# Streaming the weights of an output projection through quarters of the PE array, and loading four of their rows on five DMA engines

## The chip, the cores and the metric

The kernel runs on one core of a Trainium2 chip. The metric is the device time of one execution in microseconds. Times are medians of several runs on one chip. The profile is of one execution, and its times count from the start of the profiled span, which is 1.7 to 1.9 us shorter than the device time of the same execution.

## The reference

Two branches share one input row `x` of 1024 values and are mixed by a gate. Branch A is attention with one query over a cache of 65,536 keys and values for 4 groups of heads; branch B is a small gated MLP. Both end in an output projection.

```python
# cut to what matters
q = x @ wq                                    # 32 heads of 128
o = softmax(q k^T / sqrt(128)) v              # 4 groups, 65536 keys each: 128 MB of K and V
a = o.reshape(4096) @ wo                      # wo: 4096 x 1024, 8 MB
b = (z1 * spatially_gated(z2)) @ w_out        # w_out: 1792 x 1024, 3.5 MB
out = g * a + (1 - g) * b                     # 1024 values
```

All inputs and the output are bf16. The kernel folds the gates into the vectors (`oa` for branch A, `uT` for branch B), so both projections accumulate into one PSUM tile.

## The kernel before

Everything is loaded by one DMA queue in program order, into five buffers of 32 KB per partition. The projection is the end of the kernel:

```python
    def load(src, shape, name):
        t = kv.tile([P, CT * P], BF16, name=name, tag="kv")     # five buffers
        ...
        nc.sync.dma_start(out=v, in_=src)
        return v
    # ... attention; the last group's V tiles, then:
    out_ps = pss.tile([P, NJ, W], FP32, name="out_ps", tag="spt")

    def project(w, n, vec, c0, first=False, last=False):
        w = w.rearrange("p c (m j) -> p c j m", j=NJ)           # NJ = 8
        for c in range(n):
            for j in range(NJ):
                nc.tensor.matmul(
                    out_ps[:, j, :], lhsT=w[:, c, j, :],        # 128 columns, every 8th
                    rhs=vec[:, c0 + c:c0 + c + 1].to_broadcast([P, W]),   # W = 64
                    start=(first and c == 0 and j == 0), stop=(last and c == n - 1),
                    skip_group_check=True)

    project(load(B_w_out..., (FC, D), "wout_t"), FC, uT, 0, first=True)   # FC = 14
    wo_view = A_wo.rearrange("(p c) n -> p c n", c=OC)          # OC = 32 rows a partition
    c0 = 0
    for split in WO_SPLIT:                                      # ((8, 8), (6, 4, 3, 2, 1))
        t = kv.tile([P, CT * P], BF16, name="wo_t", tag="kv")
        ...
        for n in split:
            nc.sync.dma_start(out=t[:, c0 - b:c0 - b + n, :], in_=wo_view[:, c0:c0 + n, :])
            project(t[:, c0 - b:c0 - b + n, :], n, oa, c0, last=(c0 + n == OC))
            c0 += n
    out_sb = const.tile([P, NJ], BF16, name="out_sb")
    nc.vector.tensor_copy(out=out_sb[:], in_=out_ps[:, :, 0])
    nc.sync.dma_start(out=out..., in_=out_sb[:])
```

Each partition holds 32 rows of `wo`, of 2 KB each. One such row in all 128 partitions is 256 KB; I call it a chunk. In the text above, "four rows" are four chunks, 1 MB.

## Time and profile before

| | before |
|---|---|
| device time, median | 394.09 us |
| span of the profile | 392.5 us |
| last `wo` transfer landed | 388.06 us |
| the cast after the last matmul starts | 389.96 us |
| from there to the end of the span | 2.54 us |

The page of the kernel before, in part. The row DMA gives in 40 slices of the span the mean busy share of the 16 DMA engines in tenths, GB/s what they moved; q8 is the queue that fetches instructions. In the lines of groups stand: line, engine, operation, tiles, shapes, count, then busy time in us and the mean ns of one, then the idle time before them.

```profile
span 392.5 us, 11905 instructions
...
DMA  8999999999999999999999999999999999999971
GB/s 331 435 429 441 426 424 432 432 427 422 424 440 427 426 422 431 424 432 429 426 427 431 429 436 428 426 426 432 432 427 429 429 427 427 429 431 428 412 328 73
...
q8 instruction: 43, 0.70, 0.7%
...
HBM read 162.01 MB, written 0.00 MB: 413 GB/s over the span
...
L430 PE MATMUL out_ps<-oa,wo_t 128*128 128x64 bf16 x256 | 15.7, 229 | 0.6 <-DMA wo_t<-in_A_wo_dram 0.6
L430 PEld LDWEIGHTS <-wo_t 128*128 128x128 bf16 x256 | 15.6, 171 | 0.7 <-DMA wo_t<-in_A_wo_dram 0.7
...
L449 DVE CAST out_sb<-out_ps 128x8 bf16<-128x8 f32 x1 | 0.2, 167 | 25.1 <-PE out_ps L430 25.1
```

The DMA is busy in every slice but the last two, at about 430 GB/s in most of them. The weight loads of the projection, of 128 columns that lie 16 bytes apart, take 171 ns each; those of adjacent columns take 100 to 104 ns here (100 for the scores, 101 for `kn`, 104 for `q`).

The end of the chain of waits of the kernel before (start in us, duration in us, engine, what, count):

```profile
336.97 41.19 DMA wo_t<-in_A_wo_dram
378.20 11.74 PE out_ps L430 x192
```

After a `wo` transfer landed at 378.16, PE worked off 192 matmuls from 378.20 on without a gap, 61 ns each, and ended at 389.94. So the last stage looks bound by PE. The table of stretches says that this is half of the truth. Its columns are: stretch and length in us; busy us (and count) of PE, of PE's weight loads, of DVE, ACT and POOL; the granted clock; the DMA share; GB/s.

```profile
368.00:373.00 5.00, 5.00 (x87) 5.00 (x86) 0.00 (x0) 0.00 (x0) 0.00 (x0) 0.66 1.00 419
373.00:378.00 5.00, 4.65 (x78) 4.54 (x76) 0.00 (x0) 0.00 (x0) 0.00 (x0) 1.00 0.98 408
378.00:380.00 2.00, 1.80 (x30) 1.80 (x31) 0.00 (x0) 0.00 (x0) 0.00 (x0) 0.57 0.64 259
380.00:382.00 2.00, 2.00 (x37) 2.00 (x36) 0.00 (x0) 0.00 (x0) 0.00 (x0) 0.58 0.55 223
382.00:384.00 2.00, 2.00 (x37) 2.00 (x36) 0.00 (x0) 0.00 (x0) 0.00 (x0) 1.00 0.50 206
384.00:386.00 2.00, 2.00 (x37) 2.00 (x36) 0.00 (x0) 0.00 (x0) 0.00 (x0) 1.00 0.48 185
386.00:388.00 2.00, 2.00 (x37) 2.00 (x36) 0.00 (x0) 0.00 (x0) 0.00 (x0) 1.00 0.10 39
388.00:390.00 2.00, 1.93 (x33) 1.82 (x31) 0.04 (x1) 0.00 (x0) 0.00 (x0) 1.00 0.00 0
```

From 378 on, only half of the DMA engines still work: the share is 0.5, at half the GB/s. The completion increments that the trace records for each transfer show the same: an ordinary transfer has sixteen, as many as the core has DMA engines, and I read them as one per engine. For the last chunk they come at 378.3 to 379.7 (seven engines), 382.5 (one), 385.9 to 386.4 (six) and 387.9 and 388.1 (two). An engine moves its 16 KB share of a chunk in 0.61 to 0.65 us; eight engines are simply late, by a lag that grows through the run (the increments of one transfer are 2.2 us apart at 49 us, 5.2 at 195 and 9.8 at the end). DMA therefore ends only 1.9 us before PE. Neither can be shortened alone by much.

### The profile page before, as it was taken

Reading aid. Unit: us, or ns where it says so; the run is one execution under the profiler, and the core shown is the slowest. Engines: PE = TensorE matmul, PEld = TensorE weight load, DVE = VectorE, ACT = ScalarE, POOL = GpSimd, SP = SyncE. Lnnn points to the kernel's source line nnn. Section 1 sums busy time; section 2 is a strip of 40 time slices with the busy share of each in tenths; the row PEclk is TensorE's granted clock in tenths of the full one; section 3 lists DMA queues with packets and bytes.
Section 4 is the critical chain, followed back from the end, with each engine's and each line's share of the span. In section 5 each row is a group of like instructions: output and inputs, shape, how many; then the busy total and the mean of one; then the engine's idle time right before and its main releaser. Section 6 shows DMA issues by size and latency. Waiting matters only on the chain.

```text
span 392.5 us, 11905 instructions
## 1 busy us (share of the span) xinstructions
PE 299.9 (76%) x5539; PEld 255.0 (65%) x5539; DVE 160.0 (41%) x316; ACT 122.2 (31%) x139; POOL 1.0 (0%) x9
## 2 busy tenths in 40 slices
PE   0774379887889985979884969689949797544697
PEld 0764379887888865857774858468738683311697
DVE  3011047574685541538551526367514357201100
ACT  1000036543594431424631423237404243100000
POOL 1000000000000000000000000000000000000000
PEclk9999999999999996999996989989978898955889
DMA  8999999999999999999999999999999999999971
GB/s 331 435 429 441 426 424 432 432 427 422 424 440 427 426 422 431 424 432 429 426 427 431 429 436 428 426 426 432 432 427 429 429 427 427 429 431 428 412 328 73
DMA packets 6566, 162.78 MB, mean 415 GB/s; under 512 B 884, under 2 KB 884, under 8 KB 1268
## 3 DMA queue, kind: packets, MB, share of 16 engines
q1 hardware_dynamic: 6480, 162.01, 96.6%
q8 instruction: 43, 0.70, 0.7%
q14 instruction: 7, 0.06, 0.0%
q10 hardware_dynamic: 36, 0.00, 0.0%
HBM read 162.01 MB, written 0.00 MB: 413 GB/s over the span
## 4 chain that ended last, share of the span: by engine, by line
DMA 50%; PE 42%; DVE 3%; issue 2%; ACT 1%; SPq 1%; DVEq 0%; ACTq 0%
DMA kn<-in_A_k_cache_dram 39%; PE tps L329 22%; DMA wo_t<-in_A_wo_dram 10%; PE spt L308 10%; PE o_ps L354 5%; PE out_ps L430 3%; DVE ktt L334 1%; DVE scT L291 1%; PE om_ps L372 1%; PE s_ps L362 1%; ACT scT L314 1%; ACT ktt L332 1%; SPq L85 0%; DVE o_sb L369 0%; PE nb_ps L286 0%
## 5 line engine op out<-in xcount | busy, mean ns | idle before, releaser
L329 PE MATMUL tps<-ident_b,kn 128*128 128x128 bf16 x2048 | 164.7, 226 | 37.3 <-DMA kn<-in_A_k_cache_dram 35.7
L329 PEld LDWEIGHTS <-kn 128*128 128x128 bf16 x2048 | 124.5, 101 | 62.8 <-DMA kn<-in_A_k_cache_dram 39.3
L334 DVE COPY ktt<-tps 128x1024 bf16<-128x1024 bf16 x171 | 116.4, 689 | 113.4 <-PE tps L329 112.6
L332 ACT COPY ktt<-tps 128x1024 bf16<-128x1024 bf16 x85 | 86.0, 1012 | 163.8 <-PE tps L329 163.8
L308 PE MATMUL spt<-qT,ktt 128*128 128x64 bf16 (+7 forms) x2048 | 104.0, 194 | 6.8 <-issue 6.7
L308 PEld LDWEIGHTS <-ktt 128*128 128x128 bf16 x2048 | 87.0, 100 | 8.4 <-issue 8.1
L354 PE MATMUL o_ps<-vt,scT 128*32 128x512 bf16 x512 | 51.9, 432 | 14.9 <-DMA vt<-in_A_v_cache_dram 14.9
L354 PEld LDWEIGHTS <-scT 128*32 128x32 bf16 x512 | 15.3, 100 | 26.7 <-issue 21.0
L314 ACT CAST scT<-spt 128x512 bf16<-128x512 f32 x32 | 18.8, 588 | 16.1 <-PE spt L308 16.1
L316 DVE TENSOR_TENSOR mxr<-scT,mxr 128x512 bf16<-128x512 bf16 x24 | 10.2, 426 | 20.3 <-ACT scT L314 18.9
L295 ACT ACTIVATE scT<-scT 128x1024 bf16<-128x1024 bf16 x16 | 16.4, 1059 | 4.9 <-DVE scT L291 4.9
L430 PE MATMUL out_ps<-oa,wo_t 128*128 128x64 bf16 x256 | 15.7, 229 | 0.6 <-DMA wo_t<-in_A_wo_dram 0.6
L430 PEld LDWEIGHTS <-wo_t 128*128 128x128 bf16 x256 | 15.6, 171 | 0.7 <-DMA wo_t<-in_A_wo_dram 0.7
L193 PE MATMUL z_ps<-xT,win_t 128*128 128x18 bf16 x224 | 13.7, 211 | 1.8 <-DMA win_t<-in_B_w_in_dram 1.3
L193 PEld LDWEIGHTS <-win_t 128*128 128x128 bf16 x224 | 13.7, 158 | 1.8 <-DMA win_t<-in_B_w_in_dram 1.4
L362 PE MATMUL s_ps<-scT,ones_b 128*32 128x512 bf16 x32 | 13.4, 418 | 0.0
L369 DVE COPY o_sb<-o_ps 128x512 f32<-128x512 f32 x4 | 2.7, 684 | 26.0 <-PE o_ps L354 26.0
L245 PE MATMUL q_ps<-xT,wq_t 128*128 128x1 bf16 x256 | 7.1, 165 | 7.6 <-DMA wq_t<-in_A_wq_dram 7.6
L245 PEld LDWEIGHTS <-wq_t 128*128 128x128 bf16 x256 | 7.0, 104 | 7.8 <-DMA wq_t<-in_A_wq_dram 7.8
L291 DVE TENSOR_TENSOR scT<-scT,negm 128x1024 bf16<-128x1024 bf16 x16 | 10.7, 683 | 0.2
L449 DVE CAST out_sb<-out_ps 128x8 bf16<-128x8 f32 x1 | 0.2, 167 | 25.1 <-PE out_ps L430 25.1
L430 PE MATMUL out_ps<-uT,wout_t 128*128 128x64 bf16 x112 | 6.9, 235 | 3.2 <-DMA wout_t<-in_B_w_out_dram 3.2
(87 smaller groups left out, 57.0 us busy)
## 6 DMA issues: line engine op xcount, KB each, us to landing
kn<-in_A_k_cache_dram SPq DMA_DIRECT2D x16, 4096.0 KB, 30.2
vt<-in_A_v_cache_dram SPq DMA_DIRECT2D x16, 4096.0 KB, 32.3
wq_t<-in_A_wq_dram SPq DMA_DIRECT2D x2, 4096.0 KB, 34.7
win_t<-in_B_w_in_dram SPq DMA_DIRECT2D x2, 3584.0 KB, 15.3
wo_t<-in_A_wo_dram SPq DMA_DIRECT2D x2, 2048.0 KB, 35.1
wout_t<-in_B_w_out_dram SPq DMA_DIRECT2D x1, 3584.0 KB
wo_t<-in_A_wo_dram SPq DMA_DIRECT2D x1, 1536.0 KB
wo_t<-in_A_wo_dram SPq DMA_DIRECT2D x1, 1024.0 KB
```

The source lines that it names most:

```text
L193: nc.tensor.matmul(z_ps[:, hf * FC + f, :], lhsT=w[:, hf, f, :], rhs=xT[:, i * KH + c:i * KH + c + 1].to_broadcast([P, zw]), start=(i == 0 ...
L245: nc.tensor.matmul(q_ps[:, h:h + 1], lhsT=w[:, c % KH, h * DH:(h + 1) * DH], rhs=xT[:, c:c + 1], start=(c == 0 and h == 0), stop=(c == KC ...
L291: nc.vector.tensor_tensor(out=blk, in0=blk, in1=negm[:].unsqueeze(1).to_broadcast([P, CT, REP]), op=ALU.add)
L295: nc.scalar.activation(out=blk, in_=blk, func=ACT.Exp, scale=SCALE)
L308: nc.tensor.matmul(spt[g][:, o:o + n], lhsT=ktt[:, j * P:(j + 1) * P], rhs=qT[:, g * REP:g * REP + n], start=True, stop=True, skip_group_c ...
L314: nc.scalar.copy(out=blk, in_=spt[g][:].rearrange("p (c h) -> p c h", h=REP))
L329: nc.tensor.transpose(tps[:, i * P:(i + 1) * P], kn[:, u * TG + i, :], ident_b[:])
L332: nc.scalar.copy(out=ktt[:], in_=tps[:])
L334: nc.vector.tensor_copy(out=ktt[:], in_=tps[:])
L354: nc.tensor.matmul(o_ps[g][t * Q:(t + 1) * Q, :], lhsT=scT[g][:, cg:cg + VC, :].rearrange("p c h -> p (c h)"), rhs=vt[:, lo:lo + VC, :].re ...
L362: nc.tensor.matmul(s_ps[g][gs, :], lhsT=ones_b[:, :Q], rhs=scT[g][:, cg:cg + CPS, :].rearrange("p c h -> p (c h)"), start=(cg == 0), stop= ...
L430: nc.tensor.matmul(out_ps[:, j, :], lhsT=w[:, c, j, :], rhs=vec[:, c0 + c:c0 + c + 1].to_broadcast([P, W]), start=(first and c == 0 and j ...
```

## The change

The intent has two parts. First, PE: let the weight rows be the moving operand, 256 columns at a time, in four column quarters of the array that work side by side, with the broadcast vector as the stationary operand. There are then 4 matmuls a chunk in place of 8, and no strided weight loads. Second, DMA: let a transfer over 125 partitions carry most of four chunks. I counted on it to run on 5 engines, so that the other eleven, the late ones among them, would have less to do.

```diff
-WO_SPLIT = ((8, 8), (6, 4, 3, 2, 1))
+WO_SPLIT = ((16,), (4, 6, 3, 2, 1))
+UNEVEN = 1
+ODD = 125
@@
-    out_ps = pss.tile([P, NJ, W], FP32, name="out_ps", tag="spt")
+    NQ = P // Q
+    NO = D // NQ
+    out_ps = pss.tile([P, NO], FP32, name="out_ps", tag="spt")
@@
-            for j in range(NJ):
+            for t in range(NQ):
                 nc.tensor.matmul(
-                    out_ps[:, j, :], lhsT=w[:, c, j, :],
-                    rhs=vec[:, c0 + c:c0 + c + 1].to_broadcast([P, W]),
-                    start=(first and c == 0 and j == 0), stop=(last and c == n - 1),
+                    out_ps[t * Q:(t + 1) * Q, :],
+                    lhsT=vec[:, c0 + c:c0 + c + 1].to_broadcast([P, Q]),
+                    rhs=w[:, c, t * NO:(t + 1) * NO],
+                    start=(first and c == 0), stop=(last and c == n - 1),
@@
-        for n in split:
-            nc.sync.dma_start(out=t[:, c0 - b:c0 - b + n, :], in_=wo_view[:, c0:c0 + n, :])
+        for i, n in enumerate(split):
+            cuts = (0, ODD, P) if split is WO_SPLIT[-1] and i < UNEVEN else (0, P)
+            for p0, p1 in zip(cuts, cuts[1:]):
+                nc.sync.dma_start(out=t[p0:p1, c0 - b:c0 - b + n, :],
+                                  in_=wo_view[p0:p1, c0:c0 + n, :])
@@
-    out_sb = const.tile([P, NJ], BF16, name="out_sb")
-    nc.vector.tensor_copy(out=out_sb[:], in_=out_ps[:, :, 0])
-    nc.sync.dma_start(out=out.rearrange("o t (p j) -> (o t p) j", j=NJ), in_=out_sb[:])
+    out_sb = const.tile([P, NO], BF16, name="out_sb")
+    nc.vector.tensor_copy(out=out_sb[:], in_=out_ps[:])
+    nc.sync.dma_start(out=out.rearrange("o t (q n) -> (o t q) n", n=NO), in_=out_sb[::Q, :])
```

More of the change, by code (lines that the diff above doesn't have):

```diff
@@ L56 @@
     OC = HD // P
-    NJ = D // P
     QD = P // H
@@ L421 @@
         rest(v_units(G - 1, j, load_kv(A_v_cache, G - 1, j, "vt")))
-    out_ps = pss.tile([P, NJ, W], FP32, name="out_ps", tag="spt")
+    NQ = P // Q
+    NO = D // NQ
+    out_ps = pss.tile([P, NO], FP32, name="out_ps", tag="spt")
     def project(w, n, vec, c0, first=False, last=False):
-        w = w.rearrange("p c (m j) -> p c j m", j=NJ)
         for c in range(n):
-            for j in range(NJ):
+            for t in range(NQ):
                 nc.tensor.matmul(
-                    out_ps[:, j, :], lhsT=w[:, c, j, :],
-                    rhs=vec[:, c0 + c:c0 + c + 1].to_broadcast([P, W]),
-                    start=(first and c == 0 and j == 0), stop=(last and c == n - 1),
+                    out_ps[t * Q:(t + 1) * Q, :],
+                    lhsT=vec[:, c0 + c:c0 + c + 1].to_broadcast([P, Q]),
+                    rhs=w[:, c, t * NO:(t + 1) * NO],
+                    start=(first and c == 0), stop=(last and c == n - 1),
                     skip_group_check=True)
```

## The prediction

> **What bounds the kernel now.** Up to about 378 us it is the DMA: the page gives 413 GB/s of HBM reads over the span and a DMA row of 9s to the 38th slice. The tail is different. The chain of waits ends with a wo transfer landing at 378.20 us, then 192 `out_ps` matmuls back to back for 11.7 us (61 ns a pair), then the 0.17 us cast and 2.3 us for the output DMA. The table of stretches shows DMA running out meanwhile: share 0.98 at 373-378, then 0.64, 0.55, 0.50, 0.48 and 0.10 in two-microsecond steps to 388. The completion increments of the trace say why: of 16 engines, seven finish their share of the last transfers by 379.1-379.7, one at 382, eight at 385.3-388.1 (one chunk = one row of wo per partition, 256 KB; 0.615 us per 16 KB share). The spread grows through the run, in steps of about 1.5 us with 43 instruction fetches of 16 KB (queue q8), which seem to fall on the same engines. So two things end late: PE at 389.96 us, and DMA at 388.06 us, on half its engines. They nearly hide each other; removing one alone gains at most about 1.4 us.
>
> **What the change does.**
> 1. PE. Weight rows become the moving operand. Per chunk: 8 loads of 128 strided columns (171 ns each, against 100 ns for the contiguous loads of q and scores) become 4 loads of 32 columns and 4 matmuls of 256 columns in four column quarters, which overlap. The `o_ps` matmuls have this form with 512 columns and take 0.43 us per four at a granted clock of 0.5; so I estimate 0.11 to 0.22 us per chunk instead of 0.49. PE work for 32 chunks falls from 16 us to 4-7 us and hides behind the DMA.
> 2. DMA balance. A 1 MB transfer over 125 partitions: [...] Those five get 200 KB (208 KB on three) in place of 64 KB, about +5.4 us; the other eleven lose 2.46 us. If the five are among the seven early ones, finishes become about 383.5 (five), 376 and 379 (three), 383 (six) and 384.9 (the last two); the final chunk lands near 385.5.
> 3. PE instruction rows fall from 10,995 to 10,627, about one fetch fewer.
> 4. Added: the cast covers 256 columns, about 0.4 us instead of 0.17. The output is 4 rows of 512 B; about the same 2.3 us. Two 8-chunk transfers become one of 16, so PE starts wo later; harmless as PE is faster.
>
> **Sum.** PE end = 385.5 + about 0.5 = 386.1 instead of 389.96; minus 0.25 for the cast: -3.6 us. I shade it for the risk below: 390.5 us, 80% range 388.8 to 392.7. Chances: faster by over 2% 0.03, within 2% 0.95, slower 0.02.
>
> **Right or wrong in the profile.** PE should now wait for wo DMA before the last groups, `out_ps` busy about 5-9 us in all; the gap between the last wo landing and the last matmul about 0.5 us (1.9 before); DMA share near 0.9 until about 383; finishing spread 4-6 us (excluding engines left out) instead of 9.8; last landing near 385.5.
>
> **What would make it wrong.** [...] five engines writing into all partitions slow the others, DMA still ends near 388, and the time is about 392.5. If the five are not early engines, the last landing is later, about 392, and nothing is gained. Cold-clock matmuls slower than estimated would leave PE trailing by up to 1 us.

The sum: the last landing at 385.5, plus 0.5 to the end of PE, is 386.1 (as rounded there) for 389.96, less 0.25 for the cast, -3.6 us. But its 385.5 rests on the five engines and on their normal rate, so up to the run it was my estimate.

## The result, and the profile after

| | before | after |
|---|---|---|
| device time, median | 394.09 us | 400.81 us |
| range | 393.97 to 394.17 | 400.74 to 401.3 |
| ratio after / before | | 1.0173 (95% interval 1.0156 to 1.0191) |
| span of the profile | 392.5 us | 399.4 us |
| last `wo` transfer landed | 388.06 us | 395.83 us |
| the cast after the last matmul starts | 389.96 us | 396.32 us |

The kernel became slower by 1.7%, outside the predicted range of 388.8 to 392.7. It is still within 2%, to which the prediction gave 0.95, but on the other side. The profile after is of the slowest of its four executions (401.3 us), so its times lie up to 0.5 us above those of the others.

The page after, the same lines:

```profile
span 399.4 us, 11537 instructions
...
DMA  8999999999999999999999999999999999999981
GB/s 334 451 420 418 428 446 431 418 423 432 424 433 432 427 425 422 432 438 432 422 420 436 433 436 418 422 435 433 429 425 425 428 431 436 422 425 418 220 254 66
...
q8 instruction: 42, 0.69, 0.7%
...
L432 PE MATMUL out_ps<-wo_t,oa 128*32 128x256 bf16 x128 | 8.0, 414 | 18.4 <-DMA wo_t<-in_A_wo_dram 18.3
...
L432 PEld LDWEIGHTS <-oa 128*32 128x32 bf16 x128 | 5.4, 136 | 21.1 <-issue 20.2
...
L455 DVE CAST out_sb<-out_ps 128x256 bf16<-128x256 f32 x1 | 0.4, 425 | 31.1 <-PE out_ps L432 31.1
```

PE did nearly what was expected of it: the matmuls on `wo` are busy for 8.0 us (4 to 7 were estimated) and idle for 18.4, almost all of it waiting for DMA. The cast takes 0.43 us. What is new is a hole in the row of GB/s: 220 and 254 near the end, while the row DMA still says 9 and 8. The end of the chain of waits now runs on DMA until 395.24, with 0.6 us of matmuls behind it:

```profile
323.65 24.85 DMA vt<-in_A_v_cache_dram
348.51 46.68 DMA wo_t<-in_A_wo_dram
395.24 0.62 PE out_ps L432 x8
```

The table of stretches after (the same columns as before):

```profile
368.00:373.00 5.00, 1.94 (x39) 1.39 (x29) 0.00 (x0) 0.00 (x0) 0.00 (x0) 0.50 1.14 286
373.00:378.00 5.00, 0.00 (x0) 0.00 (x0) 0.00 (x0) 0.00 (x0) 0.00 (x0) 0.50 0.98 206
378.00:380.00 2.00, 0.00 (x0) 0.00 (x0) 0.00 (x0) 0.00 (x0) 0.00 (x0) 0.50 1.05 226
380.00:382.00 2.00, 0.00 (x0) 0.00 (x0) 0.00 (x0) 0.00 (x0) 0.00 (x0) 0.50 0.66 138
...
384.00:386.00 2.00, 1.71 (x36) 1.43 (x39) 0.00 (x0) 0.00 (x0) 0.00 (x0) 0.50 0.78 268
...
388.00:390.00 2.00, 1.05 (x16) 0.66 (x16) 0.00 (x0) 0.00 (x0) 0.00 (x0) 0.50 0.80 330
...
392.00:394.00 2.00, 1.49 (x28) 1.01 (x29) 0.00 (x0) 0.00 (x0) 0.00 (x0) 0.50 0.07 30
394.00:396.00 2.00, 1.56 (x24) 0.84 (x23) 0.00 (x0) 0.00 (x0) 0.00 (x0) 0.50 0.08 25
```

From 368 to 380, the engines are as busy as ever (share near 1; a share over 1 means that packets overlap the edge of a stretch) and move two thirds (286 for 419 GB/s) and then half (206 for 408) of what they moved. The packet records say how. In the ordinary stream a packet of 32 KB takes 1.21 us, one of 12 KB 0.46 and one of 8 KB 0.31. From 370 to 382 they take 2.33, about 0.9 and 0.62 us. That holds for the packets of the 125-partition transfer (8 KB), and as well for the 32 KB and 12 KB packets beside them: at 376 us sixteen packets are in flight, five of 8 KB, eight of 32 KB and three of 6 KB (these at about 0.47 us, normally 0.23). The next question is what in the change does this.

### The profile page after: what moved, and what is told of

Same layout as the page of the kernel before. It is cut to its first block, busy times and chain, and to the rows that moved or that the text cites. A ratio compares the mean times of both kernels' runs of the same rounds, so it can differ in the third digit from the quotient of the medians.

```text
span 399.4 us, 11537 instructions
## 1 busy us (share of the span) xinstructions
PE 289.7 (73%) x5355; PEld 240.1 (60%) x5355; DVE 160.2 (40%) x316; ACT 122.1 (31%) x139; POOL 1.0 (0%) x9
## 4 chain that ended last, share of the span: by engine, by line
DMA 63%; PE 32%; DVE 2%; issue 1%; ACT 1%; SPq 0%; DVEq 0%; ACTq 0%
DMA kn<-in_A_k_cache_dram 45%; PE tps L330 19%; DMA wo_t<-in_A_wo_dram 12%; PE spt L309 8%; DMA vt<-in_A_v_cache_dram 6%; PE o_ps L355 4%; DVE ktt L335 1%; ACT ktt L333 1%; PE om_ps L373 0%; SPq L86 0%; PE s_ps L363 0%; DVE scT L292 0%; PE out_ps L432 0%; ACT scT L315 0%; DVE o_sb L370 0%
## 5 line engine op out<-in xcount | busy, mean ns | idle before, releaser
L355 PE MATMUL o_ps<-vt,scT 128*32 128x512 bf16 x512 | 53.9, 450 | 15.2 <-DMA vt<-in_A_v_cache_dram 15.2
L432 PE MATMUL out_ps<-wo_t,oa 128*32 128x256 bf16 x128 | 8.0, 414 | 18.4 <-DMA wo_t<-in_A_wo_dram 18.3
L432 PEld LDWEIGHTS <-oa 128*32 128x32 bf16 x128 | 5.4, 136 | 21.1 <-issue 20.2
L373 PE MATMUL om_ps<-o_sb,pick 128*32 128x128 f32 x32 | 5.0, 310 | 3.1 <-DVE o_sb L370 3.1
```

The lines of the kernel that those rows point to most:

```text
L355: nc.tensor.matmul(o_ps[g][t * Q:(t + 1) * Q, :], lhsT=scT[g][:, cg:cg + VC, :].rearrange("p c h -> p (c h)"), rhs=vt[:, lo:lo + VC, :].re ...
L432: nc.tensor.matmul(out_ps[t * Q:(t + 1) * Q, :], lhsT=vec[:, c0 + c:c0 + c + 1].to_broadcast([P, Q]), rhs=w[:, c, t * NO:(t + 1) * NO], st ...
```

## The experiments

My first theory, A, was that the five-engine transfer costs all of the loss. Its rival, B, was that the new matmul form does, with its long idle times (the granted clock is 0.50 for the rest of the kernel after). Undoing one part at a time tells them apart.

### e1_stream_even: the change without the five-engine transfer

```diff
-UNEVEN = 1
+UNEVEN = 0
```

> The changed kernel with its four rows of wo loaded over all 128 partitions again (matmul form, split and output of the change kept). Theory A (the five-engine transfer costs all of the loss): wo lands without a stretch of half rate, last landing 386.5 to 388, last matmul about 0.5 us later instead of 1.9 us, cast 0.42 us; about 392.9 us, 1.2 us below the kernel before. Rival B (the new matmul form, with its idle and cold PE, costs the time): still close to 400 us.

Measured: 393.0 us (392.76 to 393.47), against 393.96 for the kernel before on the same chip; ratio 0.9975, interval 0.9959 to 0.9992. Theory A holds and B falls. The table of stretches of this run shows the full rate until 378 although PE's clock is 0.50 here too:

```profile
368.00:373.00 5.00, 2.16 (x43) 1.62 (x33) 0.00 (x0) 0.00 (x0) 0.00 (x0) 0.50 0.99 419
373.00:378.00 5.00, 0.00 (x0) 0.00 (x0) 0.00 (x0) 0.00 (x0) 0.00 (x0) 0.50 0.96 399
378.00:380.00 2.00, 1.97 (x40) 1.71 (x43) 0.00 (x0) 0.00 (x0) 0.00 (x0) 0.50 0.65 272
...
382.00:384.00 2.00, 0.49 (x12) 0.16 (x4) 0.00 (x0) 0.00 (x0) 0.00 (x0) 0.85 0.49 202
...
386.00:388.00 2.00, 1.57 (x24) 0.84 (x23) 0.00 (x0) 0.00 (x0) 0.00 (x0) 0.50 0.08 25
```

The last landing is at 387.8, and the cast starts at 388.32. Against the kernel before, that is 1.6 us earlier, but the tail from there is 2.94 us in place of 2.54 (the wider cast, and an output DMA whose issue takes 0.65 us in place of 0.35). The net gain is 1.0 us, about what the prediction gives to removing PE's lag alone.

### e2_oldmm_uneven: the five-engine transfer without the new matmuls

```diff
 # the kernel before, with
-WO_SPLIT = ((8, 8), (6, 4, 3, 2, 1))
+WO_SPLIT = ((16,), (4, 6, 3, 2, 1))
 # and the loop over cuts (0, 125, 128) of the change
```

> The kernel before, its matmuls and output kept, with the split and the 125-partition transfer of the change alone. Theory A: DMA rate falls to about 210 GB/s for 15 us from 368 on, last landing near 395.8 as in the changed kernel; PE keeps up, since landings are spread out, and the kernel takes 400 to 402 us. Rival B: about 394 us.

Measured: 404.28 us (403.61 to 404.67), ratio 1.0258. The last transfer landed at 396.3, as expected, but the time is 2.3 us above my expectation: I had thought that PE would keep up. The timeline of this run (start, length, engine, operation, count, idle time before it and its releaser) shows why it does not:

```profile
384.73 15.45 PEld L432 LDWEIGHTS <-wo_t 128*128 128x128 bf16 x256 [11.13 <-DMA wo_t<-in_A_wo_dram]
384.74 15.56 PE L432 MATMUL out_ps<-oa,wo_t 128*128 128x64 bf16 x256 [11.02 <-DMA wo_t<-in_A_wo_dram]
400.33 0.17 DVE L454 CAST out_sb<-out_ps 128x8 bf16<-128x8 f32 x1 [35.15 <-PE out_ps L432]
```

The one 16-chunk transfer is itself delayed to 384.7, and from there the old matmuls need 15.6 us for all 32 chunks. So the new form is worth 3.5 us where landings are late and bunched, and 1 us where they are not.

### e3_stream_oldsplit: the new matmuls with the old split

```diff
 # as e1_stream_even, with
-WO_SPLIT = ((16,), (4, 6, 3, 2, 1))
+WO_SPLIT = ((8, 8), (6, 4, 3, 2, 1))
```

> The new matmul form and output with the split of the kernel before (8, 8, 6, 4, 3, 2, 1) and no five-engine transfer. Theory A: within 0.3 us of the run with one 16-row transfer, about 392.9 us, because PE is ahead of the DMA in both. If the single 16-row transfer is what keeps PE from starting in time, this one is faster by up to 1 us.

Measured: 393.12 us (393.07 to 393.28), ratio 0.9977. The split does not matter (0.12 us).

### e4_probes: which transfers halve the stream

What about the 125-partition transfer halves every engine? I put six extra loads into an otherwise unchanged kernel and read packet times.

```diff
+    def probe(kind):        # one after every second K tile from group 1 on
+        t = kv.tile([P, CT * P], BF16, name="probe_t", tag="kv")
+        w = t[:].rearrange("p (c n) -> p c n", n=D)
+        # "odd":       w[0:125, 0:4]          <- wo_rows[0:125, 0:4]
+        # "odd_dense": the same partitions    <- 1 MB of K without gaps
+        # "own":       w[r:20:4, 0:12]        <- wo_rows[r:20:4, 0:12],     r = 0..3
+        # "pair":      w[64 + r:84:4, 0:12]   <- wo_rows[r:20:4, 0:12],     r = 0..3
+        # "heap":      w[5r:5r + 5, 0:12]     <- wo_rows[5r:5r + 5, 0:12],  r = 0..3
+        # "seven":     w[0:112, 0:4]          <- wo_rows[0:112, 0:4]
```

> The kernel before with six extra loads into an unused tile, one about every 40 us in the middle of the stream, to be read from packet times (normal: 1.21 us for 32 KB, 0.31 us for 8 KB, 0.92 us for 24 KB). The result stays right; the time is not compared. (1) 125 partitions of wo, 8 KB each, as in the change; (2) the same partitions from one dense megabyte of K; (3) five partitions 0, 4, 8, 12, 16 at a time (then 1, 5, ... and so on), 24 KB each[...]; (4) the same rows into partitions 64, 68, ... 80 and so on[...]; (5) five adjacent partitions at a time; (6) 112 partitions[...]. Theory A1 (writing into partitions that other engines are writing slows both): packets double in 1, 2, 4, 5 (most in 5) and 6, and stay normal in 3. Rival A2 (the read pattern of wo on five engines): they double in 1, 3, 4 and 5, not in 2. Rival A3 (any transfer on five engines halves the stream): they double in 1 to 5, not in 6.

No trace records which engine writes which partition. What the theories took for that was my assumption. What can be read is how long packets take for each choice of the partitions that a transfer writes. By the "own" partitions I mean those that I assumed the same engines to write in every ordinary transfer: in this run five partitions in steps of four within 0 to 19. The name says no more than that.

Measured, medians over the part of each probe in which its engines were all at work:

| probe | assumed own? | probe's packets | 32 KB packets beside them |
|---|---|---|---|
| odd: 125 partitions of `wo` | no | 8 KB: 0.62 us (normal 0.31) | 2.34 us (normal 1.21) |
| odd_dense: same, source without gaps | no | 8 KB: 0.62 us | 2.34 us |
| own: 0, 4, 8, 12, 16, ... | yes | 24 KB: 0.91 us (normal) | 1.21 us |
| pair: 64, 68, ... 80, ... | no | 24 KB: 1.86 us | 2.41 us |
| heap: five adjacent | mostly no | 24 KB: about 1.4 us | 1.3 to 1.9 us, by the part taken |
| seven: 112 partitions of `wo` | mostly no | 8 KB: 0.60 us | 2.30 us |

Stretches of this run before and during the first probe:

```profile
84.00:88.00 4.00, 3.92 (x92) 3.92 (x93) 3.02 (x5) 1.70 (x3) 0.00 (x0) 1.00 1.09 414
88.00:92.00 4.00, 2.57 (x62) 2.45 (x60) 1.52 (x3) 1.17 (x2) 0.00 (x0) 1.00 0.95 205
92.00:96.00 4.00, 4.00 (x99) 4.00 (x97) 3.09 (x5) 2.46 (x4) 0.00 (x0) 1.00 1.08 240
```

Rival A2 (the read pattern) falls twice: a source without gaps is just as slow, and "own" and "pair" read the very same rows of `wo`, five partitions a transfer, and only "pair", which writes into partitions 64 to 83, is slow (1.86 us for 0.91). Rival A3 (any transfer on five engines) falls too: "own", with five partitions a transfer, runs at full speed. What is shown is that it matters which partitions one transfer writes together: "own" and "heap" read and write the same twenty, grouped otherwise, and take 0.91 and about 1.4 us. A1, writing into partitions that other engines are writing, is the reading that fits, but it rests on the assumption above, and no trace shows it. One detail of A1 missed: "heap", five adjacent partitions a transfer, is not the worst (about 1.4 us). And the stream ran partly dry during "own", "pair" and "heap", because each probe took one of the five buffers. When it started again, the first 32 KB packet of many engines was slow even beside "own" (up to 2.48 us, the next ones 1.21), so I repeated three of the questions.

### e6_probes: a fuller stream, nearer neighbours, fewer partitions, and nothing beside it

```diff
-NKV = 5
+NKV = 4
+    scratch = const.tile([P, 12, D], BF16, name="scratch")
+    # scratch[p0:p0 + 20:4] <- wo_rows[r:20:4, 0:12] for r = 0..3,
+    #   p0 = r, 64 + r, 32 + r, 4 + r; then scratch[64 + r:76:4] <- wo_rows[r:12:4, 0:12]
+    # after the output DMA: scratch[0:125, 0:4] <- wo_rows[0:125, 0:4]
```

> The kernel before with one buffer fewer for K and V and a scratch tile of its own for extra loads, so that the stream is fuller during them than in the first probe run; the time is not compared. All of the first five read the same rows of wo, 24 KB each (normal 0.92 us). (1) five partitions 0, 4, 8, 12, 16 and so on[...]: theory A1 0.92 us and 32 KB packets at 1.21 us. (2) partitions 64, 68, ... 80: about 1.85 us, and 32 KB packets of all engines near 2.3 us as in the first probe run[...]. (3) partitions 32, 36, ... 48: theory A1[...]: normal. [...] (4) partitions 4, 8, ... 20[...]: slow under A1. (5) three engines, partitions 64, 68, 72: slow for all if one foreign writer is enough to stall the stream[...]. (6) 125 partitions as in the change, after everything else has landed: 8 KB packets at 0.31 us if the cost needs other engines' writes at the same time, 0.62 us if it lies in the transfer itself.

Measured (24 KB packets but for the last):

| probe | probe's packets | 32 KB packets beside them |
|---|---|---|
| (1) 0 to 19, assumed own | 0.91 us | 1.21 us |
| (2) 64 to 83, as "pair" | 0.91 us | hardly any: the stream had run dry |
| (3) 32 to 51, assumed own | 0.92 us | 1.21 us |
| (4) 4 to 23 | 1.91 us | 2.42 us |
| (5) three partitions a transfer, 64 to 75 | 1.92 us | 2.45 us |
| (6) 125 partitions, all else landed | 8 KB: 0.31 us, after a first few of about 2 us | none |

```profile
84.00:88.00 4.00, 4.00 (x96) 3.89 (x92) 3.00 (x5) 2.10 (x3) 0.00 (x0) 1.00 0.97 418
88.00:92.00 4.00, 2.94 (x72) 2.82 (x68) 2.74 (x4) 1.45 (x2) 0.00 (x0) 1.00 1.04 438
...
262.00:266.00 4.00, 0.92 (x16) 0.38 (x13) 0.69 (x1) 0.57 (x1) 0.00 (x0) 1.00 1.08 260
416.00:424.00 8.00, 0.00 (x0) 0.00 (x0) 0.00 (x0) 0.00 (x0) 0.00 (x0) 0.50 0.29 121
```

The stretch 84 to 88 has the first packets of probe (1) in its last two microseconds, and 88 to 92 is nearly all probe (1): no loss. The stretch from 262 is probe (5), at 260 GB/s with a DMA share of 1.08. The last is probe (6): a share of 0.29, about five engines of sixteen, at 121 GB/s, which is about 417 GB/s for a share of 1, as in the full stream.

Probe (3) shows that partitions 32 to 51 leave the packets at their normal times as well (0.92 and 1.21 us), and probe (4) that a shift of "own" by four partitions is enough to double them (1.91 and 2.42 us). Probe (6) shows that nothing in the transfer itself is slow: its 8 KB packets took 0.31 us with nothing beside them, and 0.62 us in e4_probes beside the stream. Probe (2) is inconclusive as a repeat, but agrees with (6). Probe (5) shows that it does not need five partitions a transfer: the thirteen 32 KB packets that were in flight together with three of the probe's took 2.35 to 3.35 us, so everything in flight was slowed. How much the others lose depends on how many of the probe's packets are in flight: when single ones were left (at 1.8 to 2.0 us), nearly all 32 KB packets beside them took 1.22 to 1.37 us ("pair" of e4_probes from 245 to 249, probe (5) from 269 to 272). Why a few packets into such partitions slow all the others, no run here shows; that stays open.

### e7_own_five: nearly the same load, five partitions a transfer, into the "own" partitions

Does the cost of these writes account for the whole loss? This kernel has at the same place six transfers of five partitions, 32 KB each (960 KB in all; 192 KB an engine over five engines), but into partitions of a spare buffer that left the packets at their normal times in the probes. Its result is wrong.

```diff
-            # 125 + 3 partitions, 4 chunks
+            for p0 in (0, 1, 2, 3, 32, 33):
+                nc.sync.dma_start(out=d[p0:p0 + 20:4], in_=wo_view[p0:p0 + 20:4, :16, :])
```

> The changed kernel with its 125-partition transfer replaced, at the same place in the queue, by six transfers of five partitions [...]. The result is wrong on purpose: those four rows are not loaded where they belong. Theory A1 (writes into other engines' partitions cost the loss): DMA rate stays above 400 GB/s until 378, packets normal; but one of the five is the late one of the early eight[...], and ends near 387.0, so nothing is gained by balance either: 391.7 to 392.8 us. Rival (192 KB on five engines of sixteen is itself what delays everything): near 400 us. If all five were early, as the prediction assumed: 390.5 us.

Measured: 392.87 us (392.58 to 393.09), ratio 0.9972; the 400.81 of the change is gone, with packets at 0.46 and 1.21 us. Packets of 8 KB in a like transfer, which this run does not have, were also at their normal 0.31 us in e5_moved below, over partitions in steps of four within 0 to 63. So where these transfers write costs 7.9 us (400.81 less 392.87), the whole of the loss and of e1's distance to the change. And the balance is worth nothing here: 392.87 against 393.0 without any. The end of its chain of waits, of which the last four matmuls wait for one more landing:

```profile
378.20 8.36 DMA wo_t<-in_A_wo_dram
386.60 0.62 PE out_ps L431 x7
```

The landing at 386.56 is of the last transfer but one; the last is at 387.19, where 387.0 was expected of the one engine of the five that I took to be late already. The engine that ends last posts its increments at 379.60, 383.34, 385.28, 386.56 and 387.19, that is 0.62 to 0.65 us per chunk, so it worked without a gap. The rate expected until 378, over 400 GB/s, was missed; the reason is given under e8_own_three.

### e8_own_three: the same, three partitions a transfer

```diff
-                nc.sync.dma_start(out=d[p0:p0 + 20:4], in_=wo_view[p0:p0 + 20:4, :16, :])
+                nc.sync.dma_start(out=d[p0:p0 + 12:4], in_=wo_view[p0:p0 + 12:4, :16, :])
```

> The same [...]. The result is wrong on purpose, and 384 KB fewer are read than in the other run. [...] the late ones at 383.8 to 385.3, so the last landing is near 385.3 and the time 390.0 to 391.0 us: what the prediction promised[...]. If the late engines gain nothing from the four rows that they no longer carry: 393 us.

Measured: 390.59 us (390.4 to 391.35), ratio 0.9916, interval 0.9901 to 0.9931. The end of its chain of waits:

```profile
378.11 7.20 DMA wo_t<-in_A_wo_dram
385.35 0.62 PE out_ps L431 x8
```

That landing too is the last but one; the last is at 385.94. (The profile is of the slowest execution, 391.35 us.) With three partitions a transfer in place of five, and partitions chosen in the same way, four chunks less on the others do give 2.4 us over e1_stream_even (390.59 for 393.0), and nearly the landing that the prediction promised, 385.5. I had taken the three for early engines; the last landing, 1.25 us before that of e7_own_five, fits, but the trace gives the engines no numbers. This is not yet a faster kernel: its result is wrong, and it reads 384 KB less than e7_own_five and 448 KB less than the four chunks. In both of these runs the next `wo` transfers were also issued late (in e7_own_five one at 377.83, just after the transfer eight before it had landed at 377.81; in the kernel before all seven were issued by 358.7). The waits of the issuing queue show it for e7_own_five (10.6 us in one wait), and the DMA share from 373 to 378 was 0.79 there and 0.68 here (the first two lines below, in this order, then the wait). The engine that ended last in e7_own_five lost nothing by it; the time of e8_own_three may be a little high for it.

```profile
373.00:378.00 5.00, 0.15 (x4) 0.14 (x7) 0.00 (x0) 0.00 (x0) 0.00 (x0) 0.50 0.79 338
...
373.00:378.00 5.00, 0.23 (x8) 0.20 (x11) 0.00 (x0) 0.00 (x0) 0.00 (x0) 0.50 0.68 292
...
SPq L457 <- DMA wo_t<-in_A_wo_dram: 10.6, 1, 10.6
```

### e5_moved: an attempt to do it correctly

In the runs with wrong results the spare buffer took the load. To load the right rows with transfers of the kind that left the stream alone, rows of `wo` have to move to other partitions, and the values of `oa` with them. This version moves the last four rows of partitions 64 to 127 to partitions 0 to 63.

```diff
+    mv = A_wo.rearrange("(u h i r c) n -> h r i u c n", u=2, h=2, i=8, r=4)
+    for h in range(2):
+        for r in range(4):
+            nc.scalar.dma_start(out=moved[32 * h + r:32 * h + 32:4],
+                                in_=mv[h, r, :, :, OC - NS:, :])          # NS = 4
+    nc.tensor.matmul(oa2_ps[:], lhsT=ident_b[:, P // 2:], rhs=oa[:, OC - NS:], ...)
```

> The new matmul form without the 125-partition transfer. Instead the last four rows of wo of partitions 64 to 127 are loaded into partitions 0 to 63, beside their own last four rows, by eight transfers of eight partitions in steps of four[...]; four columns of oa are moved to partitions 0 to 63 by one small matmul. Theory A (only writes into other engines' partitions are slow): packets of these transfers stay at normal speed, the eight late engines lose 2.46 us, last landing near 385.3 against 387.8 without it, time 390.0 to 391.2 us against 393.0. Rival (moving work between engines never helps, or any transfer on fewer than 16 engines is slow): 393 us or more.

Measured: 394.0 us (393.83 to 395.28), ratio 1.0011, result correct. The packets of these transfers took 0.31 us for 8 KB, and those beside them 1.21 us for 32 KB, so for these transfers too the normal times held. The gain did not come. The completion increments show one reason: in the V tile that landed while they ran, only six of the eight early engines were delayed, and two of the eight late ones were, from 358.2 to 361.1; those two ended last, at 388.6. So the eight engines that took the extra load were not the eight early ones; two of them were late. A second reason lies beside it: three `wo` transfers were issued only between 370.6 and 381.6, where in the kernel before the last was issued by 358.7. How much each cost was not separated.

## Why the prediction was wrong

1. **What bounds the kernel before: right.** Half of the DMA engines are late, and end 1.9 us before PE. Removing PE's lag alone gave 1.0 us (e1_stream_even); the prediction allowed at most 1.4.
2. **PE: right in what it does, somewhat low in the size.** A chunk takes 0.225 us (16 chunks in 3.60 us) at the granted clock of 0.50; 0.11 to 0.22 was estimated. The 32 chunks of `wo` are busy for 8.0 us and not 4 to 7, and `out_ps` with the 14 chunks of `w_out` for 11.2 us and not 5 to 9. It costs nothing, since PE waits for DMA: the cast starts 0.49 us after the last landing; 0.5 was predicted.
3. **DMA balance: this is the step that failed**, "Those five get 200 KB (208 KB on three) in place of 64 KB, about +5.4 us; the other eleven lose 2.46 us." The sum holds only at the normal rate of an engine. Five engines did get the transfer: its completion increments are five, and three for the three leftover partitions. But beside their writes, for some 12 us, all sixteen engines ran at about half speed (32 KB: 2.33 in place of 1.21 us). Last landing: 395.83 in place of 385.5. Nearly the same load into other partitions costs none of it (e7_own_five, 392.87 us).
4. **"If the five are among the seven early ones": also false.** The five increments of the 125-partition transfer come at 382.4, 383.6, 384.2, 385.2 and 388.4, and the last of these engines stays last to the end, 3 us behind all others. The three of the other transfer come at 382.9 to 385.4, all before it. At normal rate I would expect its end near 387 (an estimate from e7_own_five, which, with five partitions a transfer, ended at 387.19), and the gain from balance would have been about nothing. With three partitions a transfer and normal packet times, the landing is near the promised one, 385.94 against 385.5 (e8_own_three, which reads 448 KB less than the four chunks).
5. **The risk was named and mis-sized.** The prediction said that five engines writing into all partitions might slow the others, "DMA still ends near 388", 392.5 us. That holds only if the total rate stays what it was and the gain alone is undone. The total rate fell: from 419 to 286 and from 408 to 206 GB/s in the same stretches. That term was put at 2 us (392.5 against the 390.5 of the sum) and measured 7.9. The 390.5 is the sum itself, 394.1 less 3.6; the shading for this risk that the text announces is not in it.
6. **Tail: the sign was right, the size small.** From the start of the cast to the end it is 3.07 us after and 2.54 before, +0.53 and not +0.25; the issue of the output DMA of four rows takes 0.62 in place of 0.35 us.
7. **Fetches: right in number**, 42 in place of 43. (The profile counts 11,078 PE instructions before and 10,710 after; the prediction's counts differ from these, but their difference of 368 is the same.) That they are what makes eight engines late fits the steps of the lag (in the kernel before about 1.5 us each; a fetch took 0.93 to 1.11 us there), but no run tested it.

The sum, in medians: 394.0 (before), -1.0 for the new matmuls (e1_stream_even), -0.1 for the balance (e7_own_five), +7.9 for where the transfer over 125 partitions writes, gives 400.8.

The version that beats both kernels is the change without its five-engine transfer, 393.0 us, by 0.25%. A correct version of e8_own_three would have to move rows of `wo` to the few partitions that its transfers wrote (18, within 0 to 11 and 32 to 41); it was not built.

## What to carry to other kernels

A busy DMA row with low GB/s (share 0.98 at 206 GB/s) was here the sign of packets that take twice as long (2.33 us for 1.21): read the rate and the time per packet, not the share. Before a transfer gets an odd number of partitions, to choose its engines or for any other reason, time its packets, and those beside them, with the stream running: here three packets into partitions 64 to 75 were enough to double the packet times of all that was in flight (2.35 to 3.35 us for 1.21), and the five of the 125-partition transfer halved the stream (206 GB/s for 408), while five packets into partitions 0 to 19 in steps of four cost nothing (0.91 us, and 1.21 beside them). Balance by the completion times of the very engines that will get the work, not by how many of the sixteen look early.
